# One exponential instead of two ScalarE passes, and new places in the engine queues, in a fused four-layer kernel

## The chip, the cores and the metric

The kernel runs on one NeuronCore of one Trainium2 chip. The metric is the device time of one execution in microseconds. A ratio is the mean time of one kernel's runs over that of the other's from the same rounds, so it is not quite the ratio of the medians that are quoted.

In the lines of the profile, PE is TensorE (matmuls), PEld its weight loads, DVE VectorE, ACT ScalarE, POOL GpSimd, SP the engine that issues the transfers. "L661" is line 661 of the kernel in question; the change shifts line numbers, so a table below pairs them.

## The reference

```python
def _A_ref(x, wqkv, wo):                       # 32 heads of 32 channels
    q, k, v = heads(x @ wqkv)
    phi = lambda t: jnp.where(t > 0, t + 1, jnp.exp(t)) + 1e-6
    pq, pk = phi(q), phi(k)
    kv = einsum("bhsd,bhse->bhde", pk, v);  z = pk summed over s
    num = einsum("bhqd,bhde->bhqe", pq, kv)
    den = einsum("bhqd,bhd->bhq", pq, z)[..., None] + 1e-6
    return merge_heads(num / den) @ wo

def _B_ref(x, w_gate, w_up, w_down):
    return ((x @ w_gate) * (x @ w_up)) @ w_down

x = x + _A_ref(_layernorm(x)); x = x + _B_ref(_layernorm(x))   # S 2048, D 1024, F 3584
x = x + _A_ref(_layernorm(x)); x = x + _B_ref(_layernorm(x))   # the same weights again
```

## The kernel before

All engines run instruction lists that are put together in program order, with waits on semaphores of the others. So the place at which the program writes an instruction is its place in that engine's queue, and in the traces what waits at the head of ScalarE's or VectorE's queue holds up what is written behind it. In the kernel before, ScalarE stands 2.81 us at a LayerNorm activation that starts at 274.02 us; the copy behind it, whose matmuls had ended by 273.16, starts at 275.16. VectorE stands 1.00 us at a normalisation that starts at 72.35 us; the step of phi behind it, whose input was there at 69.62, starts at 72.81. Both are shown in the next section, and runs e6 and e11 below show what such places cost here.

A layer A has four stages: projections of K and Q with phi, one tile of 128 tokens at a time; G (normalised tokens against phi(K)) with the product kvT behind it; the held Q projections of the last two tiles and the product of kvT with the output weights; the y loop (output projection, residual, and LayerNorm of the next layer). A layer B has two passes, each of 28 gate/up units and a down stage. Gate/up and down both use a seven-product block scheme whose sums of weight blocks are made in the first layer B and kept in scratch memory.

```python
def phi_evac(bank, dst_ap, dst_rng):                         # phi of a 128x512 PSUM bank
    P.add("act", activation(etmp[r], psb(bank), AF.Relu, scale=-1.0))
    P.add("act", activation(etmp[r], etmp[r], AF.Exp, scale=-1.0))
    P.add("dve", tensor_scalar(etmp[r], etmp[r], 1e-6, op0=ALU.add))
    P.add("dve", scalar_tensor_tensor(dst_ap, psb(bank), C1, etmp[r], op0=ALU.add, op1=ALU.max))

def ln_a(i): ...    # DVE: bn_stats x2, bn_aggr; POOL: +eps, pow(-0.5)   (L408, L410, L411, L413)
def ln_b2(...):     # on_act: DVE L419 (in ln_b1), then ACT L425;  else: DVE tensor_scalar L428

def lnstep(i):                                               # LayerNorm in the projections
    lnp.need(i)                  # tile i normalised and transposed, now
    lnp.advance(i + 1, i + 1)    # statistics and normalisation of the next, back to back
...
def norm(i):                                                 # denominator of a tile
    pbuf = pbufs[i % 2]          # pbufs[1] shares its place with etmp and with ysb
    # DVE: x*zb -> pbuf; reduce; +1e-6; reciprocal.  POOL: pbuf*(1/den) -> asb.  SP: transpose
...
proj_q(*held[0])
kvt(2 * KT - 1)                  # ends in the mask of kvT on DVE
...
for i in range(NST):                                         # the y loop
    if na[0] < NST:
        norm(tok[na[0]]); na[0] += 1                         # last two denominators: i = 0, 1
    ...
    y_grp(tok[i], 0, i)          # PE; then DVE adds the PSUM bank to x
    nxt.b2_one()                 # LayerNorm of the next layer: normalise on ACT
    y_grp(tok[i], 1, i)          # PE; ACT copies PSUM to ysb; POOL adds
```

Of the kernel before, what the change touches and what calls it, by code (L numbers as in the profile page):

```python
# [7 lines left out]
AF = mybir.ActivationFunctionType  # L8
# [172 lines left out]
def build_kernel(nc, A_x, A_wqkv, A_wo, B_w_gate, B_w_up, B_w_down, out):  # L181
    _, S, D = A_x.shape
    F = B_w_gate.shape[1]
    NST, NSB, KT, NG, NFT, NDH = S // 128, S // 512, D // 128, D // 128, F // 128, D // 512
    NJ = NFT // 2
# [4 lines left out]
    PE_WARM = 10  # L190
    C1 = 1.0 + 1e-6
    NHOLD = 2
    NPE_T = 6
    NNORM = 14

    SZ_W = KT * D * 2
# [29 lines left out]
    O_WQ = RA + NST * D * 2  # L226
# [60 lines left out]
    with ExitStack() as es:  # L287
# [54 lines left out]
        def psb(b):  # L342
            return ps[:, b, :]
# [26 lines left out]
        def r_x(i, lo=0, hi=D):  # L370
            return [(O_X + (i * D + lo) * 2, O_X + (i * D + hi) * 2)]
# [4 lines left out]
        def r_pk(i, h):  # L376
            return R(O_PK + (h * NST + i) * 1024, 1024)
# [163 lines left out]

        def phi_evac(bank, dst_ap, dst_rng):
            r = e_cnt[0] % 3
            e_cnt[0] += 1
            er = R(O_E[r], 2048)
            P.add("act", lambda e: e.activation(etmp[r], psb(bank), AF.Relu, scale=-1.0), prd=[bank], wr=er)  # L546
            P.add("act", lambda e: e.activation(etmp[r], etmp[r], AF.Exp, scale=-1.0), rd=er, wr=er)  # L547
            P.add("dve", lambda e: e.tensor_scalar(out=etmp[r], in0=etmp[r], scalar1=1e-6, scalar2=None, op0=ALU.add),  # L548
                  rd=er, wr=er)
            P.add("dve", lambda e: e.scalar_tensor_tensor(out=dst_ap, in0=psb(bank), scalar=C1, in1=etmp[r], op0=ALU.add, op1=ALU.max),  # L550
                  prd=[bank], rd=er, wr=dst_rng)
# [100 lines left out]
        def layer_A(lnp, nxt, first):  # L652
            kq_i = [0]
            tok = lnp.order

            def proj(w, base, i, h, dst, r_dst):
                bank = B_KQ[kq_i[0] % len(B_KQ)]
                kq_i[0] += 1

                def fn(e):  # L660
                    return [e.matmul(psb(bank), xnT[:, k, i * 128:(i + 1) * 128], w[:, k, h * 512:(h + 1) * 512],  # L661
                                     start=(k == 0), stop=(k == KT - 1)) for k in range(KT)]
                P.add("pe", fn, rd=r_xT(i * 128, (i + 1) * 128) + r_w(base, h * 512, (h + 1) * 512), pwr=[bank])
                phi_evac(bank, dst, r_dst)

            def proj_k(i, h):
                proj(wk, O_WK, i, h, pk[:, h, i, :], r_pk(i, h))
                za, pa = zacc[:, h * 512:(h + 1) * 512], pk[:, h, i, :]
                rz_ = R(O_ZACC + h * 2048, 2048)
                if i == tok[0]:  # L670
                    P.add("pool", lambda e: e.tensor_copy(za, pa), rd=r_pk(i, h), wr=rz_)
                else:
                    P.add("pool", lambda e: e.tensor_tensor(out=za, in0=za, in1=pa, op=ALU.add),  # L673
                          rd=r_pk(i, h) + rz_, wr=rz_)

            def proj_q(i, h):
                proj(wq, O_WQ, i, h, x_res[:, i, h * 512:(h + 1) * 512], r_x(i, h * 512, (h + 1) * 512))

# [16 lines left out]

            def lnstep(i):
                if i < NST:
                    lnp.use_dma = (not first) or i >= NPE_T
                    lnp.need(i)
                    lnp.use_dma = False  # L700
                    lnp.advance(i + 1, i + 1)

            lnstep(0)
            seq = [("k", i) for i in range(NHOLD)]
            for i in range(NHOLD, NST):
                seq += [("k", i), ("q", i - NHOLD)]
            for kind, i in seq:
                for h in range(2):
                    (proj_k if kind == "k" else proj_q)(tok[i], h)
                    if h == 0 and kind == "k":  # L710
                        lnstep(i + 1)
                if kind == "k" and not first:
                    for t in ([tok[i - 2]] if 2 <= i < NST - 1 else tok[i - 2:] if i == NST - 1 else []):
                        dma(xr[:, t, :], nscr[t * 128:(t + 1) * 128, :], r_xr(t), KNL[t], rd=R(V_XN + t * 32, 32))
                if kind == "k" and i == NST - 1:
                    for c in range(NDH):
                        load_w("v", c)
                    for c in range(NDH):
                        load_w("o", c)
# [57 lines left out]
            for n in range(2 * KT):  # L777
# [12 lines left out]
                if n >= 2 and na[0] < NNORM:  # L790
                    norm(tok[na[0]])
                    na[0] += 1
            proj_q(*held[0])
            kvt(2 * KT - 1)
            proj_q(*held[1])
            for g in range(4, 8):
                wprod(g, [0, 4, 1, 3][g - 4], g % 2 == 0)
            proj_q(*held[2])
            for g in range(4, 8):
                wprod(NG + g, [0, 2, 1, 3][g - 4], g % 2 == 0)  # L800
            proj_q(*held[3])

# [16 lines left out]
            nxt.use_dma = True  # L819
            nxt.on_act = True  # L820
            ring_begin(first)
            for _ in range(3):
                ring_issue()
            for i in range(NST):
                if na[0] < NST:
                    norm(tok[na[0]])
                    na[0] += 1
                elif RG["n"] < NR:
                    ring_issue()
                nxt.step_t(1)  # L830
                nxt.b1_one()
                if i >= 2:
                    nxt.start(i - 2)
                y_grp(tok[i], 0, i)
                nxt.b2_one()
                y_grp(tok[i], 1, i)
                if nxt.t_next >= 8 and RG["tq"] is None:
                    RG["tq"] = t_ops(0)
                if RG["tq"]:
                    RG["tq"].pop(0)()  # L840
# [3 lines left out]
        def layer_B(lnp, nxt, first):  # L844
            is_last = nxt is None
            lnp.use_dma = True
            lnp.on_act = True
            lnp.need(7)
            for f in t_ops(0) if RG["tq"] is None else RG["tq"]:
                f()  # L850
            if not is_last:
                nxt.use_dma = True
                nxt.on_act = True

# [72 lines left out]
            def gateup(ps_, ticks):  # L927
                prev = None
                jit = first and ps_ == 0
                for u in range(NU):  # L930
# [18 lines left out]
                    prev = cur  # L949
                prev[1]()  # L950
                prev[3]()
                ring_issue()

            def down(ps_, ticks):
                i0 = ps_ * 8
# [18 lines left out]
                for qi, q in enumerate(DPROD):  # L974
# [6 lines left out]
                    for t in range(4):  # L981
                        bank = (B_DX if q in "16" else B_DV)[t]
                        start = q in "1275"
                        for hf in range(2):
# [7 lines left out]
                            if t == 3:  # L992
                                ring_issue()
                        pb = psb(bank)
                        ha, hb, hc, hd = [v[:, :, t * 128:(t + 1) * 128] for v in (hA, hB, hC, hD)]
# [37 lines left out]

            wk_ = [0]
            if first:
# [11 lines left out]
            def ticks0(u):  # L1047
                if not lnp.done():
                    lnp.flush_step()
                while first and wk_[0] < 2 * NJ and wk_[0] * 24 <= u * 2 * NJ:  # L1050
                    wd_tick(wk_[0] % 2)
                    wk_[0] += 1

# [34 lines left out]

            gateup(0, ticks0)
            lnp.need(NST - 1)  # L1090
            tq = t_ops(1)
            down(0, dticks0)
            gateup(1, ticks1)
            down(1, dticks1)
            lnp.use_dma = False
# [63 lines left out]
```

## Time and profile before

| | before |
|---|---|
| time, median of the first 3 runs | 1548.3 us (1547.48 to 1548.54) |
| span of the profiled run | 1546.2 us |
| TensorE busy / idle | 1492.5 / 53.7 us |
| VectorE, ScalarE busy | 967.5, 503.3 us |

The page of the kernel before, part 1 (busy microseconds and share of the span) and two rows of part 2 (40 equal slices, tenths):

```profile
PE 1492.5 (97%) x6925; PEld 674.1 (44%) x6990; DVE 967.5 (63%) x1642; ACT 503.3 (33%) x793; POOL 246.6 (16%) x271
...
PE   8999999899999999999999799999999999999999
...
PEclk9999999999999999999999999999999999999999
```

TensorE has work nearly always, and nothing else comes near it. So a change can win only what TensorE stands still, and what it loses at a lower clock. The waits of TensorE say for whom it stood still (total us, times, longest):

```profile
PE ps L661 <- DVE arena L550: 13.9, 13, 2.8
PE ps L878 <- ACT arena L882: 12.3, 10, 2.6
PE ps L878 <- DVE arena L602: 5.2, 3, 2.5
PE ps L767 <- DVE arena L744: 4.5, 2, 2.6
PE ps L807 <- DVE arena L813: 3.9, 2, 1.9
...
PE ps L502 <- DVE arena L428: 2.9, 2, 1.7
```

L661 are the projections, L878 the gate/up units, L767 the product of kvT with the output weights, L807 the y loop. None waits for data from memory directly; TensorE waits for a PSUM bank to be emptied, or for an operand that VectorE makes.

Where the text speaks of a *break*, it means the time by which the distance between two weight loads exceeds the usual 0.216 us. The idle times in the wait lists are up to 0.4 us shorter for the same event.

Stretches in which the clock falls (columns: busy us and count per engine, granted clock, transfers):

```profile
250.00:275.00 25.00, 20.94 (x88) 8.65 (x87) 18.61 (x40) 9.53 (x13) 5.84 (x9) 0.93 0.46 117
275.00:300.00 25.00, 22.04 (x85) 9.03 (x86) 16.25 (x38) 7.74 (x14) 1.00 (x2) 0.86 0.62 177
850.00:875.00 25.00, 19.78 (x84) 8.34 (x83) 15.25 (x31) 12.71 (x20) 8.55 (x11) 0.93 0.24 64
```

A mean of 0.93 over 25 us is one stretch of 3.41 us at half clock (granted clock 0.50 from 266.43 to 269.85 us, for one), in which weight loads start every 0.427 us in place of 0.216; so it costs 1.7 us of matmul time. 0.86 is two. There are six in the run before its end, from 191.3, 266.4, 276.7, 286.9, 867.2 and 887.7 us. Each begins within, or up to 1.2 us after, an idle stretch of TensorE of 2.17 to 2.82 us.

Now the mechanism in three places. First projections, VectorE in order of time (start, duration; in brackets the idle time before and who ended it):

```profile
69.70 1.41 DVE L408 BATCH_NORM_STATS2 arena<-arena 128x6 f32<-128x512 bf16 x2
71.14 0.21 DVE L410 BATCH_NORM_AGGREGATE arena<-arena 128x2 f32<-128x12 f32 x1
72.35 0.55 DVE L428 TENSOR_SCALAR arena<-arena 128x1024 f16<-128x1024 bf16 x1 [1.00 <-POOL arena L413]
72.81 0.42 DVE L548 TENSOR_SCALAR arena<-arena 128x512 f32<-128x512 f32 x1
```

VectorE makes the statistics of a tile and then stands 1.00 us at its normalisation until GpSimd has made the inverse root. phi (L548) stands behind it: the ScalarE pass that it reads ended at 69.62 us (L547, 0.63 us from 68.99), and L548 starts at 72.81. This repeats every 7.6 us, one tile.

First gate/up units, ScalarE in order of time:

```profile
270.61 0.60 ACT L882 ACTIVATE arena<-ps 128x512 f32<-128x512 f32 x1 [3.68 <-PE ps L878]
274.02 1.24 ACT L425 ACTIVATE arena<-arena 128x1024 f16<-128x1024 bf16 x1 [2.81 <-DVE arena L419]
275.16 0.58 ACT L882 ACTIVATE arena<-ps 128x512 f32<-128x512 f32 x1
```

ScalarE stands 2.81 us at a LayerNorm activation (L425), because the scalar that it needs (L419) is deep in VectorE's queue. The copy of a PSUM bank (L882) that TensorE waits for, 2.63 us ahead of 275.79, is one place behind.

### The profile page before, as it was taken

What the parts mean: (1) busy time and instruction counts of PE and PEld (TensorE: products, weight loads), DVE (VectorE), ACT (ScalarE), POOL (GpSimd) and SP (SyncE); (2) the same over time, 40 slices, a digit from 0 to 9 for tenths busy, and PEclk for the clock granted to TensorE, in tenths of its full rate; (3) what the DMA queues carried; (4) which work ended last, traced back from release to release, by engine and by line L of the source; (5) the groups of instructions that cost most, each with busy time, mean ns of one, the idle gap of its engine ahead of it and who ended that gap; (6) DMA issues with size and microseconds to landing.
All of it is one profiled execution on the core that took longest, in us unless ns stands there. A gap on an engine that the chain in (4) does not pass through costs nothing.

```text
span 1546.2 us, 18008 instructions
## 1 busy us (share of the span) xinstructions
PE 1492.5 (97%) x6925; PEld 674.1 (44%) x6990; DVE 967.5 (63%) x1642; ACT 503.3 (33%) x793; POOL 246.6 (16%) x271
## 2 busy tenths in 40 slices
PE   8999999899999999999999799999999999999999
PEld 3444444344444444444444344444444444444444
DVE  6887868678766475545576668775545563544553
ACT  5663334333310143330057533453333002333200
POOL 4443644000000010000033337440000000000000
PEclk9999999999999999999999999999999999999999
DMA  6124655587874798554371366746565456655443
GB/s 218 35 52 140 143 129 116 179 268 256 267 232 143 229 244 219 175 160 137 128 223 41 85 168 151 196 92 181 166 179 163 156 170 208 177 177 167 144 162 107
DMA packets 300645, 254.42 MB, mean 165 GB/s; under 512 B 102288, under 2 KB 266384, under 8 KB 300560
## 3 DMA queue, kind: packets, MB, share of 16 engines
q1 hardware_dynamic: 300560, 253.27, 56.1%
q8 instruction: 55, 0.90, 0.3%
q14 instruction: 30, 0.25, 0.0%
HBM read 195.04 MB, written 34.60 MB: 149 GB/s over the span
## 4 chain that ended last, share of the span: by engine, by line
PE 79%; DVE 11%; issue 4%; ACT 3%; POOL 2%; DMA 1%; SPq 0%; DVEq 0%; POOLq 0%; ACTq 0%
PE ps L878 41%; PE ps L988 22%; PE ps L807 6%; PE ps L661 5%; PE ps L727 4%; DVE arena L550 3%; DVE arena L548 2%; DVE arena L408 1%; DVE arena L681 1%; DVE arena L684 1%; DMA arena<-in_B_w_down_dram 1%; DVE arena L599 1%; ACT arena L425 1%; POOL arena L413 1%; ACT arena L882 1%
## 5 line engine op out<-in xcount | busy, mean ns | idle before, releaser
L878 PE MATMUL ps<-arena 128*128 128x512 f16 x3136 | 685.4, 381 | 17.5 <-ACT arena L882 12.3
L602 DVE SCALAR_TENSOR_TENSOR arena<-ps,arena 128x512 f16<-128x512 f32 (+2 forms) x536 | 365.0, 689 | 437.3 <-PE ps L988 160.8
L878 PEld LDWEIGHTS ps<-arena 128*128 128x128 f16 (+1 forms) x3136 | 306.0, 98 | 396.3 <-ACT arena L882 21.4
L882 ACT ACTIVATE arena<-ps 128x512 f32<-128x512 f32 x336 | 200.4, 596 | 551.4 <-PE ps L878 550.6
L988 PE MATMUL ps<-arena 128*128 128x512 f16 (+1 forms) x1548 | 337.4, 379 | 1.1
L661 PE MATMUL ps<-arena 128*128 128x512 bf16 x1003 | 228.3, 384 | 16.0 <-DVE arena L550 13.9
L988 PEld LDWEIGHTS ps<-arena 128*128 128x128 f16 x1568 | 153.4, 98 | 185.0
L599 DVE TENSOR_TENSOR arena<-arena 128x512 f16<-128x512 f16 (+3 forms) x416 | 222.6, 556 | 17.0 <-DMA arena<-in_B_w_down_dram 9.9
L661 PEld LDWEIGHTS ps<-arena 128*128 128x128 f16 x1024 | 99.6, 99 | 140.3 <-DVE arena L550 20.3
L807 PE MATMUL ps<-arena 128*128 128x512 bf16 x502 | 111.0, 379 | 4.8 <-DVE arena L813 3.9
L727 PE MATMUL ps<-arena 128*128 128x512 bf16 x499 | 114.2, 379 | 0.6
L411 POOL TENSOR_SCALAR arena<-arena 128x1 f32<-128x1 f32 x64 | 14.3, 224 | 554.8 <-DVE arena L410 554.6
L425 ACT ACTIVATE arena<-arena 128x1024 f16<-128x1024 bf16 x48 | 59.5, 1239 | 132.2 <-DVE arena L419 119.7
L546 ACT ACTIVATE arena<-ps 128x512 f32<-128x512 f32 x128 | 76.0, 594 | 64.3 <-PE ps L661 37.9
L690 POOL TENSOR_TENSOR arena<-arena 128x1024 f16<-128x1024 f32 x32 | 80.0, 2499 | 89.2 <-DVE arena L688 88.0
L673 POOL TENSOR_TENSOR arena<-arena 128x512 f32<-128x512 f32 x60 | 74.3, 1240 | 121.9 <-DVE arena L550 121.9
L548 DVE TENSOR_SCALAR arena<-arena 128x512 f32<-128x512 f32 x128 | 63.4, 495 | 47.5 <-ACT arena L547 46.8
L408 DVE BATCH_NORM_STATS2 arena<-arena 128x6 f32<-128x512 bf16 x128 | 88.2, 689 | 6.6 <-DMA arena<-in_A_x_dram 4.3
L550 DVE SCALAR_TENSOR_TENSOR arena<-ps,arena 128x512 bf16<-128x512 f32 x128 | 88.5, 692 | 4.4
L547 ACT ACTIVATE arena<-arena 128x512 f32<-128x512 f32 x128 | 80.7, 630 | 4.1
L807 PEld LDWEIGHTS ps<-arena 128*128 128x128 f16 x512 | 49.8, 98 | 65.8 <-DVE arena L813 4.9
L727 PEld LDWEIGHTS ps<-arena 128*128 128x128 f16 x512 | 49.2, 98 | 55.7
(42 smaller groups left out, 395.3 us busy)
## 6 DMA issues: line engine op xcount, KB each, us to landing
arena<-s_scratch SPq DMA_DIRECT2D x84, 512.0 KB, 4.5
arena<-in_B_w_gate_dram SPq DMA_DIRECT2D x56, 512.0 KB, 3.9
arena<-in_B_w_up_dram SPq DMA_DIRECT2D x56, 512.0 KB, 3.8
arena<-t_scratch SPq DMA_DIRECT2D x32, 896.0 KB, 4.8
arena<-in_B_w_down_dram SPq DMA_DIRECT2D x24, 896.0 KB, 4.6
s_scratch<-arena SPq DMA_DIRECT2D x28, 512.0 KB, 6.3
arena<-in_A_wqkv_dram SPq DMA_DIRECT2D x12, 1024.0 KB, 7.8
arena<-in_A_x_dram SPq DMA_DIRECT2D x31, 256.0 KB, 4.5
```

The lines of the kernel that those rows point to most:

```text
L408: P.add("dve", (lambda h: lambda e: e.bn_stats(st[j][:, 6 * h:6 * h + 6], x_res[:, i, (D // 2) * h:(D // 2) * (h + 1)]))(h), rd=r_x(i, (D ...
L547: P.add("act", lambda e: e.activation(etmp[r], etmp[r], AF.Exp, scale=-1.0), rd=er, wr=er)
L548: P.add("dve", lambda e: e.tensor_scalar(out=etmp[r], in0=etmp[r], scalar1=1e-6, scalar2=None, op0=ALU.add), rd=er, wr=er)
L550: P.add("dve", lambda e: e.scalar_tensor_tensor(out=dst_ap, in0=psb(bank), scalar=C1, in1=etmp[r], op0=ALU.add, op1=ALU.max), prd=[bank], ...
L599: P.add("dve", lambda e: e.tensor_tensor(out=out, in0=a, in1=b, op=op), rd=rd, wr=wr, prd=prd)
L602: P.add("dve", lambda e: e.scalar_tensor_tensor(out=out, in0=a, scalar=sc, in1=b, op0=ALU.mult, op1=op1), rd=rd, wr=wr, prd=prd)
L661: return [e.matmul(psb(bank), xnT[:, k, i * 128:(i + 1) * 128], w[:, k, h * 512:(h + 1) * 512], start=(k == 0), stop=(k == KT - 1)) for k ...
L727: return [e.matmul(psb(bank), xr[:, t, j * 128:(j + 1) * 128], pk[:, h, t, :], start=(t == 0), stop=(t == NST - 1)) for t in range(NST)]
L807: return [e.matmul(psb(bank), xnT[:, g, i * 128:(i + 1) * 128], wp[:, g, dh * 512:(dh + 1) * 512], start=(g == 0), stop=(g == NG - 1)) for ...
L878: P.add("pe", lambda e: [e.matmul(psb(bank), w[:, k, :], x[:, k, :], start=(start and k == 0), stop=(k == 3), skip_group_check=True) for k ...
L882: P.add("act", lambda e: e.activation(tm[i][0], psb(bank), AF.Copy, scale=SG), prd=[bank], wr=tm[i][1])
L988: return [e.matmul(psb(bank), hv[:, 7 * hf + k, t * 128:(t + 1) * 128], w[:, k, :], start=(start and hf == 0 and k == 0), stop=(hf == 1 an ...
```

## The change

The intent: free ScalarE of one of its two passes per phi, and take each of these waits from the head of a queue. The new phi is the same function: max(t, 0) + min(exp t, 1) + 1e-6 equals t + 1 + 1e-6 for t above 0 and exp t + 1e-6 below. Its core:

```diff
-def phi_evac(bank, dst_ap, dst_rng):
+def phi_evac(bank, dst_ap, dst_rng, eng):
-    P.add("act", activation(etmp[r], psb(bank), AF.Relu, scale=-1.0))
-    P.add("act", activation(etmp[r], etmp[r], AF.Exp, scale=-1.0))
-    P.add("dve", tensor_scalar(etmp[r], etmp[r], 1e-6, op0=ALU.add))
-    P.add("dve", scalar_tensor_tensor(dst_ap, psb(bank), C1, etmp[r], ALU.add, ALU.max))
+    P.add("act", activation(etmp[r], psb(bank), AF.Exp))
+    P.add(eng,   tensor_scalar(etmp[r], etmp[r], 1.0, 1e-6, op0=ALU.min, op1=ALU.add))
+    P.add("dve", scalar_tensor_tensor(dst_ap, psb(bank), 0.0, etmp[r], ALU.max, ALU.add))
 ...  (eng is "dve" everywhere)
+def lnstep(i, h):                 # first layer: statistics two tiles ahead of the transpose
+    if h == 0:
+        if lnp.n < NST: lnp.start(lnp.n)
+        lnp.b_one()
+    else:
+        lnp.use_dma = i + 1 >= NPE_T
+        lnp.step_t(1)
 ...  # second layer A: one lnp.flush_step() per tile of Q projections, but the first
-proj_q(*held[0])
+ph = proj_q(*held[0])             # matmuls now, phi later
 kvt(2 * KT - 1)
+ph()
 ...  # y loop
     if na[0] < NST:
-        norm(tok[na[0]]); na[0] += 1
+        if i % 3 == 2:            # last two denominators at i = 2 and 5
+            norm(tok[na[0]]); na[0] += 1
 ...  # layer B
-lnp.on_act = True;  nxt.on_act = True
+lnp.on_act = False; nxt.on_act = False       # normalise on VectorE
 ...  # the last two products of a gate/up pass are put behind 7 matmuls of the down stage
-    while first and wk_[0] < 2 * NJ and wk_[0] * 24 <= u * 2 * NJ:
-        wd_tick(wk_[0] % 2); wk_[0] += 1
+    if first and wdn[0] < NJ and wdn[0] * 24 <= u * NJ:
+        wd_tick(1)                # sums and store of the block that is there
+        wd_tick(0)                # load of the next
+# and one wd_tick(0) ahead of the first unit
```

More of the change, by code (lines that the diff above doesn't have):

```diff
@@ L190, in build_kernel @@
     PE_WARM = 10
-    C1 = 1.0 + 1e-6
     NHOLD = 2
@@ L194, in build_kernel @@
     NNORM = 14
+    YACT = True
     SZ_W = KT * D * 2
@@ L545, in phi_evac @@
             er = R(O_E[r], 2048)
-            P.add("act", lambda e: e.activation(etmp[r], psb(bank), AF.Relu, scale=-1.0), prd=[bank], wr=er)
-            P.add("act", lambda e: e.activation(etmp[r], etmp[r], AF.Exp, scale=-1.0), rd=er, wr=er)
-            P.add("dve", lambda e: e.tensor_scalar(out=etmp[r], in0=etmp[r], scalar1=1e-6, scalar2=None, op0=ALU.add),
+            P.add("act", lambda e: e.activation(etmp[r], psb(bank), AF.Exp), prd=[bank], wr=er)
+            P.add(eng, lambda e: e.tensor_scalar(out=etmp[r], in0=etmp[r], scalar1=1.0, scalar2=1e-6, op0=ALU.min, op1=ALU.add),
                   rd=er, wr=er)
-            P.add("dve", lambda e: e.scalar_tensor_tensor(out=dst_ap, in0=psb(bank), scalar=C1, in1=etmp[r], op0=ALU.add, op1=ALU.max),
+            P.add("dve", lambda e: e.scalar_tensor_tensor(out=dst_ap, in0=psb(bank), scalar=0.0, in1=etmp[r], op0=ALU.max, op1=ALU.add),
                   prd=[bank], rd=er, wr=dst_rng)
@@ L654, in layer_A, with proj @@
             tok = lnp.order
-            def proj(w, base, i, h, dst, r_dst):
+            def proj(w, base, i, h, dst, r_dst, eng):
                 bank = B_KQ[kq_i[0] % len(B_KQ)]
@@ L663, in proj @@
                 P.add("pe", fn, rd=r_xT(i * 128, (i + 1) * 128) + r_w(base, h * 512, (h + 1) * 512), pwr=[bank])
-                phi_evac(bank, dst, r_dst)
+                return lambda: phi_evac(bank, dst, r_dst, eng)
             def proj_k(i, h):
-                proj(wk, O_WK, i, h, pk[:, h, i, :], r_pk(i, h))
+                proj(wk, O_WK, i, h, pk[:, h, i, :], r_pk(i, h), "dve")()
                 za, pa = zacc[:, h * 512:(h + 1) * 512], pk[:, h, i, :]
@@ L676, in proj_q @@
             def proj_q(i, h):
-                proj(wq, O_WQ, i, h, x_res[:, i, h * 512:(h + 1) * 512], r_x(i, h * 512, (h + 1) * 512))
+                return proj(wq, O_WQ, i, h, x_res[:, i, h * 512:(h + 1) * 512], r_x(i, h * 512, (h + 1) * 512), "dve")
             def norm(i):
@@ L694, in norm @@
                       rd=R(O_A[b], D * 2), wr=r_xT(i * 128, (i + 1) * 128), dma_sem=KTA[b])
-            def lnstep(i):
-                if i < NST:
-                    lnp.use_dma = (not first) or i >= NPE_T
-                    lnp.need(i)
-                    lnp.use_dma = False
-                    lnp.advance(i + 1, i + 1)
-            lnstep(0)
+            def lnstep(i, h):
+                if h == 0:
+                    if lnp.n < NST:
+                        lnp.start(lnp.n)
+                    lnp.b_one()
+                else:
+                    lnp.use_dma = i + 1 >= NPE_T
+                    lnp.step_t(1)
+            if first:
+                lnp.start(0)
+                lnp.b_one()
+                lnp.step_t(1)
+                lnp.start(1)
+                lnp.b_one()
+                lnp.start(2)
+            else:
+                lnp.use_dma = True
             seq = [("k", i) for i in range(NHOLD)]
@@ L708, in layer_A @@
                 for h in range(2):
-                    (proj_k if kind == "k" else proj_q)(tok[i], h)
-                    if h == 0 and kind == "k":
-                        lnstep(i + 1)
+                    if kind == "k":
+                        proj_k(tok[i], h)
+                        if first:
+                            lnstep(i, h)
+                    else:
+                        proj_q(tok[i], h)()
+                        if not first and h == 0 and i >= 1:
+                            lnp.flush_step()
                 if kind == "k" and not first:
@@ L792, in layer_A @@
                     na[0] += 1
-            proj_q(*held[0])
+            ph = proj_q(*held[0])
             kvt(2 * KT - 1)
-            proj_q(*held[1])
+            ph()
+            proj_q(*held[1])()
             for g in range(4, 8):
                 wprod(g, [0, 4, 1, 3][g - 4], g % 2 == 0)
-            proj_q(*held[2])
+            proj_q(*held[2])()
             for g in range(4, 8):
                 wprod(NG + g, [0, 2, 1, 3][g - 4], g % 2 == 0)
-            proj_q(*held[3])
+            proj_q(*held[3])()
             def y_grp(i, dh, n):
@@ L819, in layer_A @@
             nxt.use_dma = True
-            nxt.on_act = True
+            nxt.on_act = YACT
             ring_begin(first)
@@ L825, in layer_A @@
                 if na[0] < NST:
-                    norm(tok[na[0]])
-                    na[0] += 1
+                    if i % 3 == 2:
+                        norm(tok[na[0]])
+                        na[0] += 1
                 elif RG["n"] < NR:
@@ L846, in layer_B @@
             lnp.use_dma = True
-            lnp.on_act = True
+            lnp.on_act = False
             lnp.need(7)
@@ L852, in layer_B @@
                 nxt.use_dma = True
-                nxt.on_act = True
+                nxt.on_act = False
             def unit(ps_, u):
@@ L949, in gateup, with tail, down @@
                     prev = cur
-                prev[1]()
-                prev[3]()
-                ring_issue()
-            def down(ps_, ticks):
+                def tail():
+                    prev[1]()
+                    prev[3]()
+                    ring_issue()
+                return tail
+            def down(ps_, ticks, tail):
                 i0 = ps_ * 8
@@ L993, in down @@
                                 ring_issue()
+                            if qi == 0 and t == 0 and hf == 0:
+                                tail()
                         pb = psb(bank)
@@ L1032, in stash @@
                 dma(xscr[i * 128:(i + 1) * 128, :], x_res[:, i, :], R(V_X + i * 32, 32), KXS[i], rd=r_x(i))
-            wk_ = [0]
             if first:
@@ L1049, in ticks0 @@
                     lnp.flush_step()
-                while first and wk_[0] < 2 * NJ and wk_[0] * 24 <= u * 2 * NJ:
-                    wd_tick(wk_[0] % 2)
-                    wk_[0] += 1
+                if first and wdn[0] < NJ and wdn[0] * 24 <= u * NJ:
+                    wd_tick(1)
+                    wd_tick(0)
             def dticks0(q, t):
@@ L1087, in dticks1 @@
                             stash(8 + k)
-            gateup(0, ticks0)
+            if first:
+                wd_tick(0)
+            tail = gateup(0, ticks0)
             lnp.need(NST - 1)
             tq = t_ops(1)
-            down(0, dticks0)
-            gateup(1, ticks1)
-            down(1, dticks1)
+            down(0, dticks0, tail)
+            tail = gateup(1, ticks1)
+            down(1, dticks1, tail)
             lnp.use_dma = False
```

## The prediction

> **What bounds the kernel.** TensorE. The page gives it 97% busy (1492.5 us) of a 1546.2 us span; VectorE has 63%, ScalarE 33%. Weight loads start every 0.216 us in undisturbed stretches, and at that pace all matmuls would fill about 1480 us (an estimate: counts times the start-to-start time). The rest, about 69 us, is what a reordering can win: 58.7 us of breaks between weight loads, and about 10 us of half-clock time. The table by 25 us stretches grants 0.93 or 0.86 where breaks of 2.5 us and more fall (175-200, 250-300, 850-900 us), six dips of about 1.7 us each. [...]
>
> **Where the breaks are (waits, timeline), and what the change does there.**
> 1. First K/Q projections, 50-111 us: eight breaks of 0.89 us and one of 0.67, one per LayerNorm tile. VectorE stands in its queue at the normalisation until GpSimd has made the inverse root (0.22 + 0.57 us). Statistics now run a tile ahead. VectorE's load per tile (4 phi x 1.06 + LayerNorm 2.1 = 6.4 us) is under TensorE's 6.9. Gain 7. At the start itself only about 0.5: the copy of the PE transposes (1.0 us) now lies bare twice.
> 2. Masking of kvT (188 and 965 us): 2.9 + 2.3 us and one clock dip. The mask stands behind phi, which waits for a GpSimd reader of its buffer. It now goes first. Gain 6.5.
> 3. Start of the y loop (208-213, 983-987 us): 2.9 us each, VectorE busy with two denominators back to back. Spread out: gain 4.
> 4. First gate/up units, 262-286 us: 8.1 us and three dips (5.1 us); 1037-1052: 3.7 us. ScalarE's queue stands at a LayerNorm activation that waits for VectorE, and the PSUM copies stand behind it. Normalisation moves to VectorE (0.55 us for 0.21 plus 1.24 on ScalarE). Gain 14.5.
> 5. Waits for w_down (316, 360, 392 us): 6.3 us. Loads are issued one interval earlier (landing 5.3-5.8 us). Gain 5.5.
> 6. End of each gate/up pass: 4 x 1.06 us, TensorE waiting for a ScalarE copy; seven matmuls (1.5 us) now cover it. Gain 4.
> 7. Second K/Q projections, 854-887 us: 10.7 us and two dips (3.4 us); statistics, GpSimd, VectorE, ScalarE, VectorE in one round trip per tile. Now spread over steps, on VectorE. Gain 13.
>
> The phi change itself removes 128 ScalarE passes (80.7 us busy). ScalarE isn't the limit: it shortens the latency from matmul to phi by 0.63 us and is worth little, perhaps 1 us. VectorE keeps two operations per phi at the same shapes, so I expect its 0.42-0.49 and 0.69 us again. VectorE gains some 15 us of work, off the path.
>
> **Sum.** 7.5 + 6.5 + 4 + 14.5 + 5.5 + 4 + 13 = 55. New small waits take back 3 (the second denominator in the y loop still waits for a GpSimd reader).
>
> **Predicted: 1496 us, range 1485 to 1511.** Faster by over 2%: 0.90; within 2%: 0.09; slower: 0.01.
>
> **What would show the steps right.** TensorE idle under 15 us; at most one clock dip after the start; no 0.89 us series at 50-110; nothing over 1 us at 850-890 and 262-286; no wait of TensorE for the mask; ScalarE busy about 410 us; VectorE about 980.
>
> **What would make it wrong.** VectorE's queue is in order, too: if the normalisation there waits for a transpose out of its buffer, or the block sums for w_down, PSUM isn't emptied and the breaks return under VectorE's name, above all in the first gate/up units, where preparation, LayerNorm and block sums meet. If min-and-add takes longer than the single add, the first projections become VectorE-bound (6.4 of 6.9 us).

55 less 3 is 52 us, and 1548 less 52 is 1496. That VectorE's queue is in order is seen above, where phi stands behind a wait of 1.00 us. Not every break of 2.5 us and more had a dip: those ahead of 319.0 us (2.87 us) and 857.5 us (2.72 us) had none.

## The result, and the profile after

The changed kernel takes 1508.48 us (median of 4 runs, 1506.34 to 1510.12) against 1547.89 (4 runs): ratio 0.9744, 95% interval 0.9727 to 0.9761, faster by 2.6%. The time lies in the range of the prediction, 12.5 us above the predicted 1496. The four runs took 1509.0, 1510.1, 1507.9 and 1506.3 us at granted clocks of 0.999, 0.998, 1.000 and 1.000. One half-clock stretch is 0.001 of such a run, so (an estimate from these figures) they held about one, two, none and none; the profiled run is the first.

The page after, the same parts:

```profile
PE 1481.8 (98%) x6925; PEld 673.9 (45%) x6990; DVE 974.0 (65%) x1642; ACT 400.1 (27%) x643; POOL 257.9 (17%) x271
...
PE   8999999999999999999999999999999999999999
```

ScalarE is busy 103 us less. Its one pass per phi, Exp out of PSUM, takes 597 ns (L546); before, Relu out of PSUM took 594 (L546) and Exp out of SBUF 630 (L547). TensorE's idle time fell from 53.7 to 25.5 us (1507.3 less 1481.8). Its waits after:

```profile
PE ps L822 <- ACT arena L831: 4.9, 5, 2.1
PE ps L894 <- DVE arena L601: 4.8, 4, 1.6
PE ps L660 <- ACT arena L504: 3.4, 3, 1.1
...
PE ps L894 <- DVE arena L598: 1.8, 1, 1.8
```

| | before | after |
|---|---|---|
| projection matmul | L661 | L660 |
| phi: add (before), min and add (after); last step | L548; L550 | L547; L549 |
| y loop: matmul; copy on ScalarE; add on VectorE | L807; L816; L813 | L822; L831; L828 |
| gate/up: matmul; copy on ScalarE; VectorE's outputs; sums | L878; L882; L602; L599 | L894; L898; L601; L598 |
| denominator: first product on VectorE; last product on GpSimd | L681; L690 | L680; L689 |

The projections' waits for VectorE (13.9 us) and the gate/up units' for ScalarE (12.3 us) are gone. But a wait that was nearly absent before (0.4 us) leads the list: the y loop waits for its copies on ScalarE. First projections, VectorE after:

```profile
66.50 1.41 DVE L408 BATCH_NORM_STATS2 arena<-arena 128x6 f32<-128x512 bf16 x2
67.95 0.21 DVE L410 BATCH_NORM_AGGREGATE arena<-arena 128x2 f32<-128x12 f32 x1
68.08 0.49 DVE L428 TENSOR_SCALAR arena<-arena 128x1024 f16<-128x1024 bf16 x1
68.49 0.42 DVE L547 TENSOR_SCALAR arena<-arena 128x512 f32<-128x512 f32 x1
```

The normalisation (L428) now uses statistics that were made one step earlier and follows without the 1.00 us of idling. The new min-and-add (L547) has here the same 0.42 us as the single add (the means over the run are 513 ns after and 495 before), and the last step of phi took 692 ns in both (L550 before, L549 after). The clock after, in three stretches, the last one in the second y loop:

```profile
275.00:300.00 25.00, 25.00 (x117) 11.33 (x116) 20.72 (x47) 8.36 (x14) 0.00 (x0) 1.00 0.97 282
850.00:875.00 25.00, 24.89 (x119) 11.47 (x119) 13.05 (x22) 8.07 (x13) 6.56 (x5) 1.00 0.27 85
950.00:975.00 25.00, 21.81 (x95) 9.36 (x96) 15.32 (x32) 7.46 (x9) 12.16 (x18) 0.97 0.67 148
```

For every kernel (e8, which is told in the text, left out here) the traces were cut at the first weight load of each stage; the difference between the starts of two stages is the stage's time. This table carries most of what follows. (The end of each gate/up pass, 8 matmuls or 1.73 us, moved into the down stage, so these are taken together. Down stages have no breaks. Left out are: the time before the first projection, 8.5 to 9.7 us from run to run whatever the kernel; the start of the second projections and the G stages, the same in all; and the last pass, which goes as the second one does.)

| stage, us | before | after | e1 | e2 | e3 | e4 | e5 | e6 | e11 | e7 | e9 | e10 |
|---|---|---|---|---|---|---|---|---|---|---|---|---|
| first projections, first 64 matmuls | 18.2 | 18.1 | 18.1 | 17.6 | 17.6 | 18.9 | 17.6 | 17.6 | 18.1 | 18.1 | 18.1 | 15.4 |
| first projections, rest | 96.7 | 90.7 | 90.7 | 90.7 | 90.7 | 90.7 | 96.3 | 90.7 | 90.7 | 90.7 | 90.7 | 91.3 |
| first held stage | 13.1 | 8.8 | 8.8 | 8.8 | 9.0 | 9.5 | 9.4 | 8.9 | 9.1 | 8.8 | 8.8 | 9.1 |
| first y loop | 57.8 | 58.1 | 57.1 | 56.0 | 58.4 | 57.3 | 57.1 | 57.2 | 55.7 | 55.5 | 55.5 | 55.5 |
| gate/up + down, first pass | 273.5 | 262.0 | 259.3 | 261.8 | 257.7 | 260.7 | 275.1 | 272.4 | 260.5 | 257.5 | 255.6 | 255.6 |
| gate/up + down, second pass | 254.7 | 253.8 | 253.8 | 253.8 | 253.8 | 253.8 | 254.7 | 253.8 | 253.8 | 253.8 | 253.8 | 253.8 |
| second projections, rest | 103.0 | 89.8 | 89.8 | 89.8 | 89.8 | 89.8 | 97.4 | 89.8 | 89.8 | 89.8 | 89.8 | 89.8 |
| second held stage | 10.8 | 9.0 | 8.8 | 9.1 | 9.0 | 10.0 | 10.1 | 8.8 | 8.8 | 9.0 | 8.8 | 8.8 |
| second y loop | 57.8 | 60.7 | 57.2 | 58.4 | 62.0 | 62.2 | 57.1 | 60.6 | 56.3 | 55.9 | 55.6 | 56.0 |
| second layer B, first pass | 257.8 | 254.0 | 253.8 | 254.0 | 253.8 | 253.8 | 257.8 | 257.1 | 254.7 | 253.8 | 253.8 | 253.8 |
| span | 1546.2 | 1507.3 | 1499.3 | 1502.8 | 1503.9 | 1509.6 | 1535.3 | 1519.7 | 1499.4 | 1494.5 | 1492.3 | 1491.3 |
| half-clock stretches before the end | 6 | 1 | 0 | 0 | 1 | 1 | 4 | 4 | 0 | 0 | 0 | 0 |

Two rows stand out. Both y loops got longer, by 0.4 and 2.9 us, where the prediction counted on 4 us less. Of the 2.9 us, 1.7 are the one half-clock stretch of that run. And the first gate/up pass, which won the most, has 8.2 us left to win (262.0 against the 253.8 of the undisturbed pass).

### The profile page after: what moved, and what is told of

Same layout as the page of the kernel before. It is cut to its first block, busy times and chain, and to the rows that moved or that the text cites. A ratio compares the mean times of both kernels' runs of the same rounds, so it can differ in the third digit from the quotient of the medians.

```text
span 1507.3 us, 17881 instructions
## 1 busy us (share of the span) xinstructions
PE 1481.8 (98%) x6925; PEld 673.9 (45%) x6990; DVE 974.0 (65%) x1642; ACT 400.1 (27%) x643; POOL 257.9 (17%) x271
## 3 DMA queue, kind: packets, MB, share of 16 engines
q1 hardware_dynamic: 300560, 253.27, 58.4%
## 4 chain that ended last, share of the span: by engine, by line
PE 87%; DVE 6%; DMA 3%; POOL 2%; issue 1%; ACT 1%; SPq 0%; POOLq 0%; DVEq 0%; ACTq 0%
PE ps L894 42%; PE ps L1006 22%; PE ps L660 14%; PE ps L741 6%; PE ps L822 2%; DVE arena L598 1%; DMA arena<-arena 1%; DMA arena<-in_B_w_down_dram 1%; DVE arena L408 1%; DVE arena L683 1%; DVE arena L680 1%; POOL arena L689 1%; DMA arena<-in_A_wqkv_dram 1%; DVE arena L601 1%; PE ps L753 0%
## 5 line engine op out<-in xcount | busy, mean ns | idle before, releaser
L894 PE MATMUL ps<-arena 128*128 128x512 f16 x3136 | 679.9, 379 | 6.6 <-DVE arena L601 4.8
L601 DVE SCALAR_TENSOR_TENSOR arena<-ps,arena 128x512 f16<-128x512 f32 (+2 forms) x536 | 364.6, 689 | 415.9 <-PE ps L1006 154.6
L894 PEld LDWEIGHTS ps<-arena 128*128 128x128 f16 (+1 forms) x3136 | 305.4, 98 | 379.8 <-DVE arena L601 9.1
L898 ACT ACTIVATE arena<-ps 128x512 f32<-128x512 f32 x336 | 200.6, 597 | 552.8 <-PE ps L894 549.4
L598 DVE TENSOR_TENSOR arena<-arena 128x512 f16<-128x512 f16 (+3 forms) x416 | 222.7, 557 | 12.2 <-DMA arena<-in_B_w_down_dram 5.0
L660 PE MATMUL ps<-arena 128*128 128x512 bf16 x1003 | 222.4, 379 | 4.8 <-ACT arena L504 3.4
L660 PEld LDWEIGHTS ps<-arena 128*128 128x128 f16 x1024 | 99.6, 98 | 122.7 <-ACT arena L504 3.9
L546 ACT ACTIVATE arena<-ps 128x512 f32<-128x512 f32 x128 | 76.4, 597 | 232.8 <-PE ps L660 217.1
L822 PE MATMUL ps<-arena 128*128 128x512 bf16 x502 | 113.2, 383 | 6.0 <-ACT arena L831 4.9
L411 POOL TENSOR_SCALAR arena<-arena 128x1 f32<-128x1 f32 x64 | 20.7, 324 | 553.3 <-DVE arena L410 553.3
L549 DVE SCALAR_TENSOR_TENSOR arena<-ps,arena 128x512 bf16<-128x512 f32 x128 | 88.5, 692 | 4.4
L689 POOL TENSOR_TENSOR arena<-arena 128x1024 f16<-128x1024 f32 x32 | 80.2, 2507 | 60.5 <-DVE arena L687 51.0
L547 DVE TENSOR_SCALAR arena<-arena 128x512 f32<-128x512 f32 x128 | 65.6, 513 | 29.5 <-ACT arena L546 28.3
L822 PEld LDWEIGHTS ps<-arena 128*128 128x128 f16 x512 | 49.8, 99 | 69.0 <-ACT arena L831 7.6
L741 PEld LDWEIGHTS ps<-arena 128*128 128x128 f16 x512 | 49.2, 98 | 55.7
L908 ACT ACTIVATE arena<-ps 128x512 f16<-128x512 f32 x56 | 33.4, 597 | 63.3 <-PE ps L894 63.3
L832 POOL TENSOR_TENSOR arena<-arena 128x512 bf16<-128x512 bf16 x32 | 42.1, 1316 | 44.2 <-ACT arena L831 44.2
## 6 DMA issues: line engine op xcount, KB each, us to landing
arena<-in_A_x_dram SPq DMA_DIRECT2D x31, 256.0 KB, 4.9
```

The source lines that it names most:

```text
L546: P.add("act", lambda e: e.activation(etmp[r], psb(bank), AF.Exp), prd=[bank], wr=er)
L549: P.add("dve", lambda e: e.scalar_tensor_tensor(out=dst_ap, in0=psb(bank), scalar=0.0, in1=etmp[r], op0=ALU.max, op1=ALU.add), prd=[bank], ...
L598: P.add("dve", lambda e: e.tensor_tensor(out=out, in0=a, in1=b, op=op), rd=rd, wr=wr, prd=prd)
L601: P.add("dve", lambda e: e.scalar_tensor_tensor(out=out, in0=a, scalar=sc, in1=b, op0=ALU.mult, op1=op1), rd=rd, wr=wr, prd=prd)
L660: return [e.matmul(psb(bank), xnT[:, k, i * 128:(i + 1) * 128], w[:, k, h * 512:(h + 1) * 512], start=(k == 0), stop=(k == KT - 1)) for k ...
L689: P.add("pool", lambda e: e.tensor_tensor(out=asb[b].rearrange("p (h c) -> p h c", c=32), in0=pbuf.rearrange("p (h c) -> p h c", c=32), in ...
```

## The experiments

All kernels below gave the reference's result. They ran in four groups; each group shared its chip with runs of the kernel before (medians 1547.3 to 1548.5 us), and across groups ratios are compared. No run takes back the earlier statistics of the first projections (term 1 of the prediction), the earlier mask (term 2) or the covered ends of the gate/up passes (term 6) by itself; their causes are read from the traces before and after.

### e1: the last two denominators back at their old places

```diff
-    if i % 3 == 2:
-        norm(tok[na[0]])
-        na[0] += 1
+    norm(tok[na[0]])
+    na[0] += 1
```

> The changed kernel with the last two denominators put back at the first two steps of the y loop, nothing else. The y loops took 57.76 us each before and 58.14 and 60.66 us after, where 256 matmuls at 0.216 us need 55.3. Theory A (the new places of the denominators cost: the second stands behind a GpSimd reader in the middle of LayerNorm work): both y loops return to about 57.8, the dip at 973 us goes, total 3 to 4 us shorter than after. Theory B (the loss is displaced: TensorE reaches the y loop 4.2 us and 1.8 us earlier, VectorE's and GpSimd's work has not got shorter): the y loops stay at 58 us or more, first loop even longer than after, and the total does not fall.

Measured: 1501.17 us (1500.89 to 1501.40), ratio 0.9702 (0.9689 to 0.9715). The y loops are 57.1 and 57.2 us, the clock dip of the second is gone. The total fell by about 7 us, more than the 3 to 4 of theory A: the first gate/up pass is 2.7 us shorter as well. In the changed kernel it starts with a break of 2.2 us behind VectorE's block sums (the L598 wait above, 1.8 us idle), and with e1 that break is gone, because VectorE leaves the y loop with less left to do. VectorE's last add of the loop and the sums after it, in the changed kernel (TensorE loads its last weights of the loop at 245.8 us):

```profile
247.33 0.64 DVE L828 TENSOR_TENSOR arena<-ps,arena 128x512 bf16<-128x512 f32 x1
247.89 4.02 DVE L598 TENSOR_TENSOR arena<-arena 128x512 f16<-128x512 bf16 x8
```

and in e1 (last weights of the loop at 244.4 us):

```profile
243.33 0.69 DVE L828 TENSOR_TENSOR arena<-ps,arena 128x512 bf16<-128x512 f32 x1
243.94 3.89 DVE L598 TENSOR_TENSOR arena<-arena 128x512 f16<-128x512 bf16 x8
```

So VectorE ended the loop 2.2 us behind TensorE there, and 0.4 us ahead here. Theory B, that the loss had only been displaced from earlier stages, falls. The new places cost about 7 us: a part of the change that harms.

### e2 and e11: why the new places cost

In the y loop of the changed kernel, ScalarE in order of time, after the second denominator:

```profile
210.56 1.24 ACT L425 ACTIVATE arena<-arena 128x1024 f16<-128x1024 bf16 x1 [4.42 <-DVE arena L419]
212.57 0.59 ACT L831 COPY arena<-ps 128x512 f32<-128x512 f32 x1 [0.77 <-POOL arena L689]
217.16 1.24 ACT L425 ACTIVATE arena<-arena 128x1024 f16<-128x1024 bf16 x1 [4.01 <-DMA arena<-arena]
218.31 0.56 ACT L831 COPY arena<-ps 128x512 f32<-128x512 f32 x1
221.66 1.24 ACT L425 ACTIVATE arena<-arena 128x1024 f16<-128x1024 bf16 x1 [2.78 <-DMA arena<-arena]
```

It is the picture of the first gate/up units again: a LayerNorm activation (L425) stands at the head of ScalarE's queue, for 4.42, 4.01 and 2.78 us, and the copy of a PSUM bank (L831) stands behind it. The first wait is for VectorE, which is in the denominator. The later two are for transposes: the activation writes one of two buffers, and the transpose out of it is late. (From issue to landing the ten transposes at 186 to 240 us took 3.0 to 6.3 us, median 3.2.) TensorE in the same loop:

```profile
212.71 5.35 PE L822 MATMUL ps<-arena 128*128 128x512 bf16 x24 [0.29 <-DVE arena L828]
219.15 3.40 PE L822 MATMUL ps<-arena 128*128 128x512 bf16 x15 [1.09 <-ACT arena L831]
223.42 3.63 PE L822 MATMUL ps<-arena 128*128 128x512 bf16 x16 [0.87 <-ACT arena L831]
```

e2 takes away one link: the second denominator's product goes into the buffer that the y copies do not use.

```diff
-    norm(tok[na[0]])                # product in pbufs[i % 2]
+    norm(tok[na[0]], 0)             # product in pbufs[0]
```

> The changed kernel, the last two denominators at their new places, but both products in the buffer that no y copy uses, so that the second waits for no GpSimd reader and no y copy waits for it. Theory A1 (the wait for the shared buffer, 2.0 us of VectorE at 205-207 us, is the cause): the y loops fall to 55.5 to 56.5 us, total 5 us shorter than after. Theory A2 (the work itself, 3 us on VectorE and 1.9 to 2.8 us on GpSimd in the middle of LayerNorm tiles, with the transposes queued behind it, is the cause): the y loops stay within 1 us of after.

Measured: 1503.37 us, ratio 0.9716 (0.9703 to 0.9730). The y loops are 56.0 and 58.4 us: 2.1 and 2.3 us less than in the changed kernel. The first is inside the range of A1, the second is not, and 1.7 of its 2.3 us are the half-clock stretch that this run did not have. The total, 5.1 us less, is as A1 expected. The shared buffer is one part of the cause, plainly so in the first loop only.

e11 takes away another link, and moves nothing: three buffers for the normalised tile instead of two.

```diff
-O_XN = [take(D * 2) for _ in range(2)]
+O_XN = [take(D * 2) for _ in range(3)]
 ...  (n % 2 becomes n % 3 in the buffer and in the semaphore of its transpose;
 ...   the room comes from an unused end of the etmp region: take(7168) -> take(6144))
```

> The changed kernel with three buffers for the normalised tile in place of two, nothing else moved. In the y loops of the changed kernel ScalarE's normalisation waits 11.4 us for transposes out of its buffer, and the y copies that free PSUM stand behind it in ScalarE's queue. Theory S (the late denominator holds up the transposes on the queue of the transfers, and through the buffer ScalarE): with a third buffer ScalarE no longer stands there, y loops 56 to 57.5 us (58.14 and 60.66), total 3 to 5 us under the changed kernel. Theory V (VectorE's 3 us for the denominator alone, with LayerNorm statistics, keeps PSUM full): y loops within 0.7 us of the changed kernel.

Measured: 1502.86 us, ratio 0.9717 (0.9702 to 0.9731), 5.6 us less where theory S expected 3 to 5. The y loops are 55.7 and 56.3 us, so the late transposes are the way by which the denominator reached TensorE. TensorE in the first y loop of e11, as above; 141 matmul records follow without another wait:

```profile
187.91 24.34 PE L822 MATMUL ps<-arena 128*128 128x512 bf16 x110
212.53 31.25 PE L822 MATMUL ps<-arena 128*128 128x512 bf16 x141 [0.29 <-DVE arena L828]
```

VectorE's work in this loop is the same as in the changed kernel, so theory V falls. In the first loop ScalarE's waits for transposes fell from 11.4 to 3.7 us, as expected. In the second they did not fall in the profile (4.6 and 8.4 us), although TensorE no longer waits; a wait for several semaphores is put down to the last one, and in the changed kernel much of that loop's waiting stands under VectorE's name. That the second loop works in the same way is read from its time, not from its waits (and 1.7 of its 4.3 us are again the clock).

### e3: the block sums for w_down at even distances

```diff
-    if first and wdn[0] < NJ and wdn[0] * 24 <= u * NJ:
+    if first and wdn[0] < NJ and wdn[0] * 2 <= u:
```

> The changed kernel with the block sums for w_down at every second gate/up unit exactly, in place of 24 units for 14 (which puts some one unit, 6 us, apart). If the remaining breaks at 302, 335 and 377 us come from those short intervals (load not landed when its sums are due), they go: 1.79 + 0.74 + 1.93 = 4.5 us less in the first gate/up pass, and VectorE's wait for w_down falls from 5.0 to under 1 us. If VectorE is simply overloaded there, they stay or move. The break at 264 us should stay in both.

VectorE's wait for w_down in the first gate/up pass of the changed kernel:

```profile
DVE arena L598 <- DMA arena<-in_B_w_down_dram: 5.0, 3, 2.2
```

Fourteen blocks are spread over 24 units, in whole units, so the steps are mostly two units, but one unit at three places: units 6 to 7, 11 to 12 and 18 to 19. There the load, issued only after the sums of the block before, has 6 us; it needs 5.6 us to land (the median of the 13 loads of this stretch, 6.2 at most; the 4.7 in part 6 of the page is the median of the whole run). Ahead of the break at 302 us it was issued at 295.4 us, and the next sums began at 301.4, after VectorE had stood 1.37 us for it.

Measured: 1504.91 us, ratio 0.9726 (0.9713 to 0.9739). The wait is not in the list of that stretch any more, the breaks at 302, 335 and 377 us are gone, and the first pass is 4.3 us shorter; 4.5 were expected. The break at 264 us stayed, as expected. The second y loop was 1.3 us longer with nothing changed in it, which ate a part.

### e4 and e5: what the phi change is worth, on either side

e4 puts the old phi into the changed kernel; e5 puts the new phi alone into the kernel of before. The diff of both is the phi part of the change.

> The changed kernel with the old phi (Relu and Exp on ScalarE, add and max on VectorE), all new places kept. The prediction's view: the phi change is worth about 1 us, so this takes 1509 to 1510 us, projections within 1 us of after. Rival (the title's view: the saved ScalarE pass is what paid): several us longer in the two projection stages, 90.7 and 89.8 us now, towards 96.7 and 103.

> The kernel of before with the new phi alone. First projections: VectorE sets the 7.6 us period there, so within 0.5 us of the 96.7 of before. Second projections (103.0 us before): each of the four LayerNorm round trips holds two ScalarE passes fewer in a row, so 2 to 3 us shorter. Masking of kvT: the chain to the mask is 0.63 us shorter, twice. Total 3 to 5 us under before if that is all; 0 to 1 us if the phi change pays nowhere; over 10 us if it is what the whole gain rests on.

Measured: e4 1510.12 us, ratio 0.9759 (0.9746 to 0.9773), beside 0.9744 for the changed kernel. In the trace the projections after their first 64 matmuls take 90.7 and 89.8 us in both, to 0.01 us. Only the start (0.9 us) and the two held stages (0.7 and 1.0 us) are longer; the y loops and the first gate/up pass vary by 0.8 to 1.6 us either way. So in the changed kernel the headline is worth about 2 us, at the edge of what these runs resolve.

e5 took 1537.96 us, ratio 0.9935 (0.9922 to 0.9947): 10.6 us less than before, where 3 to 5 were expected, and the same change of phi. The expectation had kept "over 10" for a phi that the whole gain rests on; e4, which keeps all but 2 us of the gain with the old phi, rules that reading out. In the old order its second pass lay in the chains that stopped TensorE. The second projections are 5.6 us shorter (the round trip ScalarE, VectorE, GpSimd, VectorE, ScalarE lost a pass), the first held stage 3.6. Each of these stages lost one of its half-clock stretches with it, 1.7 us, which the expectation had not counted. The first projections are within 0.4 us, as expected: VectorE set their pace. The gains of the parts thus overlap: phi alone wins 10.6 us, and what it still adds to the new places is about 2.

### e6: the normalisation back on ScalarE, in the new order

```diff
-lnp.on_act = False; nxt.on_act = False
+lnp.on_act = True;  nxt.on_act = True
```

> The changed kernel with the normalisation in the gate/up passes and second projections put back on ScalarE, the order in the queues kept. Theory M (moving it to VectorE is what cleared the first gate/up units): the first pass grows from 175.7 us by 5 us or more with clock dips at 250-275 us, and that of the second layer from 167.7 by 2 to 3. Theory O (order alone did it): both within 1 us of after. Second projections (89.8 us): the spreading should be enough there, within 1 us under both.

Measured: 1521.58 us, ratio 0.9831 (0.9817 to 0.9844), 13 us slower than the changed kernel. The first gate/up pass is 10.4 us longer, with three dips, and that of the second layer 3.1 us. The waits of TensorE at 240 to 300 us in e6:

```profile
PE ps L894 <- ACT arena L898: 7.0, 3, 2.6
PE ps L894 <- DVE arena L598: 1.8, 1, 1.8
```

and in the changed kernel:

```profile
PE ps L894 <- DVE arena L598: 1.8, 1, 1.8
PE ps L894 <- DVE arena L601: 1.4, 1, 1.4
```

Theory M stands: the engine mattered there, not the order alone. ScalarE has idle time in plenty in that stretch (8.36 us busy of 25 in the changed kernel); it was the place at the head of its queue that cost: in e6 the activation L425 stands there for 2.34 and 2.81 us before the copies at 256.0 and 266.5 us. In the second projections neither the engine (89.8 us in both) nor phi (e4) made a difference: what is left is the spreading over the Q projections, which was not taken back alone.

### e7 to e10: a version that beats both

e7 joins what e1 to e3 taught: the denominators at i = 0 and 1, with the buffers swapped (the first uses the one that the y copies share, before any y copy; the second the free one), and sums at odd units.

```diff
-    if i % 3 == 2:
-        norm(tok[na[0]])
-        na[0] += 1
+    norm(tok[na[0]], 1 - i)
+    na[0] += 1
 ...
-    if first and wdn[0] < NJ and wdn[0] * 24 <= u * NJ:
+    if first and wdn[0] < NJ and wdn[0] * 2 + 1 <= u:
```

> A version meant to beat both: the changed kernel, with the last two denominators at the first two steps of the y loop and their buffers swapped (the first uses the one that the y copies share, before any y copy; the second the free one), and the block sums at every odd unit. Y loops 55.5 to 56 us (57.1 with the old places alone), first gate/up pass 167.5 to 169.5 us (171.3 with even units), total 1494 to 1497 us.

Measured: 1496.77 us, ratio 0.9669 (0.9656 to 0.9682). Y loops 55.5 and 55.9 us. The gate/up part of the first pass is 171.2 us, not 167.5 to 169.5: a break of 2.3 us at 259 us is left.

e8 adds a new order in all first projections: each transpose between the two halves of a K projection, so that ScalarE's copy of it lies under matmuls.

```diff
 def lnstep(i, h):
     if h == 0:
-        if lnp.n < NST: lnp.start(lnp.n)
-        lnp.b_one()
-    else:
         lnp.use_dma = i + 1 >= NPE_T
         lnp.step_t(1)
+        lnp.b_one()
+    elif lnp.n < NST:
+        lnp.start(lnp.n)
```

> As the run before it, and in the first projections each transpose goes between the two halves of a K projection, its normalisation one step earlier and the statistics after the second half, so that the 1.0 us copy of the transposes lies under a matmul group. The three breaks of 1.3 us before 20 us should shrink by 2 to 3 us in all; total 1492 to 1495 us. If VectorE falls behind there instead, breaks of TensorE behind VectorE take their place and nothing is won.

Measured: 1497.59 us, ratio 0.9675 (0.9661 to 0.9688), outside the expected 1492 to 1495 and no better than e7. The first 64 matmuls take 16.4 us instead of 18.1, but the rest 92.3 instead of 90.7: five breaks of 0.47 us came in at 72 to 101 us. What is won is given back.

e9 is e7 with the sums at even units; e10 is e9 with the order of e8 for the first two tiles alone.

```diff
-    if first and wdn[0] < NJ and wdn[0] * 2 + 1 <= u:     # e9
+    if first and wdn[0] < NJ and wdn[0] * 2 <= u:
 ...
+    if i < 2 and h == 0:                                  # e10
+        lnp.step_t(1)
+        lnp.b_one()
+    elif i < 2:
+        lnp.start(lnp.n)
-    if h == 0:
+    elif h == 0:
```

> The best version so far (1496.8 us) with the block sums at every even unit in place of every odd one. With odd units one break of 2.3 us at 259 us is left, where sums, preparation and LayerNorm meet in the second unit. Even units put the first sums into the first unit. If the lag of VectorE from the y loop made the break at 264 us in the even version (1.8 us), it is gone with the lag: first gate/up pass 168.5 to 169.5 us (171.2 with odd), total 1494 to 1495 us. If that work is too much for VectorE wherever it is put, the pass stays at 171 us and the total at 1496 to 1497 us.

> As the run before it, and the first two transposes alone set between the halves of their K projections; from the third tile on the changed kernel's order, so that the five breaks of 0.47 us that the full reordering brought at 71-100 us do not come. First part of the projections 16.4 to 17 us (18.1), the rest 90.7 us as in the changed kernel; total 1 to 1.7 us under the run before it.

Measured: e9 1494.62 us, ratio 0.9658 (0.9645 to 0.9672). Its gate/up part is 169.3 us, within the expected figure, but for another reason than expected: the break of 1.8 us is there still (now at 259 us), though the y loop leaves VectorE no lag. So the lag was not its cause; that preparation, LayerNorm and sums meet there is read from VectorE's list and was not isolated. e10 took 1493.10 us (1492.76 to 1493.71), ratio 0.9649 (0.9636 to 0.9663). Its start is 2.8 us shorter than e9's (15.4 us, where 16.4 to 17 were expected) and its rest 0.6 longer (91.3, where 90.7 was expected); in all it is 1.5 us faster. The total is as expected, but two misses of opposite sign lie under it. It is the fastest kernel, 3.5% under the kernel before and about 1% under the changed kernel. All that its TensorE waits for, beyond half a microsecond in total:

```profile
PE ps L1135 <- POOL arena L389: 3.3, 1, 3.3
PE ps L899 <- DVE arena L601: 1.4, 1, 1.4
PE ps L660 <- ACT arena L504: 1.1, 1, 1.1
```

## Why the prediction was right or wrong

It was right in kind and in range (faster, 1485 to 1511), and 12.5 us too low in its middle. That 1508.5 fell inside owes something to a range that reached 15 us to the slow side: the gains came to three quarters of the sum. Term by term, in microseconds of span, read from the stage table:

| term of the sum | predicted gain | measured |
|---|---|---|
| 1 first projections and start | 7.5 | 6.0 (0.0 of it before the 64th matmul) |
| 2 mask of kvT | 6.5 | 6.0 |
| 3 y loops | 4 | -3.3 |
| 4 + 5 first gate/up units, w_down | 14.5 + 5.5 | 13.6 |
| 6 ends of the gate/up passes | 4 | 3.4 (4 x 0.86) |
| 7 second projections | 13 | 13.2 |
| small new waits | -3 | in the rows above |
| sum | 52 | 38.9 |

Term 6 was measured in the two second passes, where nothing else changes, and taken the same for all four; row 4 + 5 is what is left of the two first passes.

- What bounds the kernel was right: TensorE, and its breaks and half-clock stretches were all there was to win. The estimate of 1480 us for the matmuls alone fits e10, whose span of 1491.3 us holds 13.4 us of idle time.
- **The step that failed is term 3, "Start of the y loop ... Spread out: gain 4".** The two denominators one after the other at the start did cost something, and the prediction saw that the second still waits for a GpSimd reader. What it left out is what stands behind it there: the LayerNorm tiles of the next layer, whose transposes, buffers and ScalarE activations form a ring. A denominator in the midst of this holds up the transposes; ScalarE stands at its normalisation and TensorE behind ScalarE's copies (e11). Putting the denominators back wins 1.0 and 3.5 us, which brings both loops 0.6 us under those of the old kernel (e1); 1.7 of the 3.5 are the half-clock stretch. The prediction had warned of breaks "under VectorE's name", above all in the first gate/up units. Those came as well (4.8 and 1.8 us of waits for L601 and L598); the y loop's came under ScalarE's name, and of these it had not warned.
- **The term that was mis-sized is 4 + 5, 20 against 13.6.** The mechanism of 4 is confirmed by e6. Of the 6.4 us missing, e3 shows 4.3: "Loads are issued one interval earlier" took the interval for constant, and it is one unit at three places. Another 2.7 us is the y loop's remainder in VectorE's queue, which the prediction did not carry over the stage border (e1). The two need not add up exactly.
- The phi change, "worth little, perhaps 1 us", was right for its place in this change (about 2 us, e4), and would have been wrong as a statement on phi by itself (10.6 us, e5). The prediction listed the moved waits first and left phi the rest, which is one of the two orders in which overlapping gains can be booked.
- Terms 1, 2, 6 and 7 were right to about 1.5 us. For term 1 the prediction's check that VectorE's 6.4 us per tile is under TensorE's 6.9 us held: after the first 64 matmuls the changed projections run without breaks.
- Of the signs: one clock dip (right in the profiled run), ScalarE about 410 us (400.1), VectorE about 980 (974.0), min-and-add at the old duration (0.42 us in the places shown; right, though the mean over the run rose from 495 to 513 ns), no series at 50 to 110 us (right), "nothing over 1 us at ... 262-286" (wrong: 1.8 us at 264), "TensorE idle under 15 us" (wrong: 25.5, and 13.4 in e10: 1491.3 less 1477.9).

## What to carry to other kernels

When an engine with much idle time holds up the bottleneck, look at what stands at the head of its queue and for whom it waits; here work that is on time on the average still put a PSUM copy behind a slow round trip, and moving it to another engine won 13 us (e6) and one more buffer 5.6 us (e11), where a shorter phi added about 2 (e4). Before an operation is put into a steady loop to spread it, follow all that queues behind it, the transfers too, and look where integer rounding makes the spacing short (4.3 us, e3). Parts of a change that shorten the same chain did not add up here (phi: 10.6 us alone, about 2 on top of the rest), so measure a part both alone and taken out.
